# Three passes for a second tile's first product, free clock-warming matmuls, and another order of all operations

## The chip, the cores and the metric

The kernel runs on one core of one Trainium2 chip. The metric is the device time of one execution in microseconds (us), as the median of several runs. Each engine of the core (TensorE, called PE; VectorE, DVE; ScalarE, ACT; GpSimd, POOL) and the queue that issues the transfers (SP) takes its own instructions in the order in which the program gives them; semaphores hold an instruction until what it needs is there.

## The reference

Two layers are applied twice in turn to x of 2048 rows and 640 columns, in float32. The first is an attention over eight earlier rows at distances 0, 2, ... 14, with 32 heads of 20; the second is an MLP with 1536 hidden features. Each is preceded by a layer norm and added to its input.

```
y = layernorm(x)
q, k, v = split(y @ wqkv)                       # 640 -> 3 * 640, 32 heads of 20
logits[s, w] = q[s] . k[s - 2 w] * 20 ** -0.5   # w = 0..7, masked where s - 2 w < 0
x = x + (softmax(logits) . v[s - 2 w]) @ wo
x = x + gelu(layernorm(x) @ w1 + b1) @ w2 + b2  # 640 -> 1536 -> 640
# the same two lines of layers once more, with the same weights
```

## The kernel before, in words

**Tiling.** The rows are split by parity and by halves into four units of 512 rows (`UNITS`); a unit has four tiles of 128 rows. With two layers there are eight unit steps, n = 0 to 7, and the first unit is n = 0. The 640 columns of q, k and v are taken in four groups g of 160.

**Products in two halves.** Each float32 operand is held as a high float16 part and a low float16 part. A product takes three passes: high by high, high by low, low by high (`PASS`), five contraction steps of 128 each, so 15 matmuls for a tile. The high part of a weight slice is made by ACT (line 434) and its low part by DVE (line 435), in `prep_q`; a group of q, k, v has three slices (g, 0), (g, 1), (g, 2).

**The first unit.** Each tile's rows are loaded (line 430), normed on DVE, POOL and DVE again (lines 561 to 563, 566, 606), and split into a high half by ACT (613) and a low half by DVE (615). For tiles 0 and 1 of the first unit PE itself transposes each half with five matmuls against an identity (`turn`, line 489) and ACT copies the result to `yT` (line 497); all other tiles are transposed by a DMA from SP (line 620). Then `qkv` makes the product of the transposed tile with a group's weights (line 654), ACT evicts it (673), and two evicted tiles are put to memory (679), from where `fetch` reads them for the attention (698). The product of tile 0 with group 0 alone is issued in three passes with needs of their own (line 661): the high half by the weights' high parts, then the low half by the high parts, then the high half by the low parts.

**Warming.** Nine operations of eight 128-column matmuls on the identity (`warm`, line 1153) compute nothing that is used. Each needs the identity and, in this kernel, the mean and variance of the first tile; that need is for the planner's order, and the matmuls themselves read the identity alone.

**What sets the order.** The program first lists all operations with engine, needs and buffers (`plan.add`). `Plan.run` then emits them in the order of the list `ORDER`, written out by number; `PLACES` gives the buffer of each use and `BESIDE` a few extra waits. So the order on each engine is fixed by `ORDER`.

Of the kernel before, what the change touches and what calls it, by code (L numbers as in the profile page):

```python
# [261 lines left out]
def sliding_dilated_then_mlp_kernel(  # L262
# [141 lines left out]
    def identity():  # L404
# [7 lines left out]
        give=["b1"])  # L412
# [822 lines left out]
```

## Time and profile before

| | us |
|---|---|
| median of 3 runs (lowest, highest) | 1145.03 (1144.39, 1145.48) |
| the profiled execution's own time | 1144.26 |
| its span, first to last instruction | 1142.5 |
| PE busy in the span | 1134.2 (99%) |
| DVE busy in the span | 1073.7 (94%) |
| ACT busy in the span | 552.5 (48%) |

A row of a timeline gives the start in us, the duration, engine, line, operation, what is written from what, and in brackets the engine's idle time before it and what ended that. Matmuls overlap in the array, so a row's duration is longer than the step from one matmul to the next.

### The profile page before, as it was taken

The numbers are of one execution on the slowest core, as the hardware profiler recorded it, in microseconds if no ns is written. First come the engines' busy times: TensorE is split into PE (matmuls) and PEld (weight loads), VectorE is DVE, ScalarE is ACT, GpSimd is POOL, SyncE is SP. The second block draws the span as 40 slices with busy tenths as digits, with TensorE's granted clock in tenths as the row PEclk, the third lists the DMA queues.
The fourth block names the chain that finished last, engine by engine and source line by source line (L and its number), as shares of the span: only waits on it lengthen the run. The fifth ranks groups of instructions, "written<-read, shape, count | busy, mean of one in ns | idle before, by whom it ended". The sixth has DMA issues, their size and how long they took to land.

```text
span 1142.5 us, 17648 instructions
## 1 busy us (share of the span) xinstructions
PE 1134.2 (99%) x6932; PEld 647.0 (57%) x6932; DVE 1073.7 (94%) x1003; ACT 552.5 (48%) x977; POOL 159.1 (14%) x98
## 2 busy tenths in 40 slices
PE   8999999999999999999999999999999999999998
PEld 5444446577654565445555654556455546566886
DVE  8899999999999999999999999999999999988482
ACT  5476434545364438423645552355447542286360
POOL 2011110311111113100213011121211200300000
PEclk9999999999999999999999999999999999999999
DMA  9999999899976675956475866674598877788856
GB/s 295 324 311 277 278 331 279 262 266 308 240 198 196 216 192 125 253 182 188 155 216 188 179 188 188 213 190 133 164 267 275 258 209 221 211 218 225 251 152 189
DMA packets 259023, 257.38 MB, mean 225 GB/s; under 512 B 138540, under 2 KB 209532, under 8 KB 258940
## 3 DMA queue, kind: packets, MB, share of 16 engines
q1 hardware_dynamic: 258940, 256.26, 78.0%
q8 instruction: 54, 0.88, 0.3%
q14 instruction: 29, 0.24, 0.1%
HBM read 175.64 MB, written 48.71 MB: 196 GB/s over the span
## 4 chain that ended last, share of the span: by engine, by line
PE 99%; DVE 0%; DMA 0%; issue 0%
PE ps L654 34%; PE ps L847 17%; PE acc L866 14%; PE ps L810 11%; PE acc L1124 9%; PE ps L1061 7%; PE acc L869 4%; PE acc L1024 3%; PE ps L1024 1%; PE acc L1153 0%; DMA xf<-in_A_x_dram 0%; PE ps L661 0%; DVE bn L561 0%; PE acc L489 0%; DVE hl L615 0%; DVE bn L562 0%
## 5 line engine op out<-in xcount | busy, mean ns | idle before, releaser
L654 PE MATMUL ps<-wq,yT 128*128 128x480 f16 x1905 | 390.4, 366 | 0.0
L654 PEld LDWEIGHTS <-yT 128*128 128x128 f16 x1905 | 185.6, 98 | 197.0
L847 PE MATMUL ps<-yT,c 128*128 128x512 f16 (+1 forms) x1080 | 204.0, 344 | 0.0
L866 PE MATMUL acc<-c,act 128*128 128x512 f16 x720 | 203.4, 379 | 0.0
L741 DVE TENSOR_TENSOR pr<-qk 128x2560 f32<-128x2560 f32 (+1 forms) x44 | 179.6, 4088 | 0.7
L767 DVE TENSOR_TENSOR pr<-sm,v 128x2560 f32<-128x2560 f32 (+1 forms) x44 | 177.1, 4032 | 0.4
L745 DVE TENSOR_REDUCE sm<-pr 128x128 f32<-128x2560 f32 (+1 forms) x44 | 176.6, 4017 | 0.0
L847 PEld LDWEIGHTS <-c 128*128 128x128 f16 x1080 | 103.8, 98 | 87.4
L673 ACT ACTIVATE ev<-ps 128x480 f32<-128x480 f32 x128 | 70.7, 564 | 162.9 <-PE ps L654 155.5
L869 PE MATMUL acc<-c,act 128*128 128x128 f16 x720 | 148.2, 219 | 0.0
L775 DVE TENSOR_TENSOR pr<-pr 128x2560 f32<-128x2560 f32 (+2 forms) x88 | 143.8, 1645 | 0.2
L810 PE MATMUL ps<-wo,yT 128*128 128x320 f16 x960 | 134.7, 299 | 0.0
L866 PEld LDWEIGHTS <-act 128*128 128x128 f16 x720 | 70.3, 98 | 80.3 <-DVE act L858 0.2
L810 PEld LDWEIGHTS <-yT 128*128 128x128 f16 x960 | 93.0, 98 | 38.1
L590 POOL TENSOR_TENSOR ln<-ln,half 128x2 f32<-128x2 f32 (+1 forms) x30 | 48.6, 1621 | 408.9 <-ACT ln L587 408.9
L1124 PE MATMUL acc<-c,wq 128*128 128x320 f16 x630 | 92.9, 299 | 0.0
L853 ACT ACTIVATE act<-ps,b 128x512 f32<-128x512 f32 (+1 forms) x72 | 43.8, 613 | 93.1 <-PE ps L847 56.0
L624 POOL TENSOR_TENSOR xf<-xf,b 128x640 f32<-128x640 f32 x28 | 58.1, 2085 | 172.9 <-DVE xf L816 36.0
L788 POOL TENSOR_TENSOR ohl<-o,ohl 128x640 f16<-128x640 f32 x24 | 44.3, 1846 | 266.6 <-ACT ohl L786 118.7
L1061 PE MATMUL ps<-yT,c 128*128 128x512 f16 x360 | 78.7, 379 | 0.0
L1124 PEld LDWEIGHTS <-wq 128*128 128x128 f16 x630 | 61.6, 98 | 24.2
L571 ACT ACTIVATE junk<-xf 128x640 f16<-128x640 f32 x56 | 41.1, 733 | 66.8 <-DVE xf L816 54.8
(137 smaller groups left out, 1145.1 us busy)
## 6 DMA issues: line engine op xcount, KB each, us to landing
c<-mw SPq DMA_DIRECT2D x180, 320.0 KB, 4.0
spill<-ev SPq DMA_DIRECT2D x64, 480.0 KB, 5.6
qk<-spill SPq DMA_DIRECT2D x32, 880.0 KB, 5.4
v<-spill SPq DMA_DIRECT2D x32, 880.0 KB, 5.7
c<-msp SPq DMA_DIRECT2D x36, 320.0 KB, 3.6
qk<-spill SPq DMA_DIRECT2D x32, 320.0 KB, 4.8
c<-mw SPq DMA_DIRECT2D x54, 160.0 KB, 3.1
mw<-c SPq DMA_DIRECT2D x24, 320.0 KB, 5.6
```

The lines of the kernel that those rows point to most:

```text
L654: nc.tensor.matmul(ps, transposed(yk)[:, a * KD + k, t * P:(t + 1) * P], wq[:, b, k, g], start=j == 0, stop=j == 3 * KD - 1)
L673: act(3 * GC, -400 + n, lambda i=i, pk=pk, ek=ek: nc.scalar.activation(tile_of(*ek)[:, :, i], tile_of(*pk)[:, :3 * GC].rearrange("p (a c) ...
L741: return nc.vector.tensor_mul(pr(pk), w[:, HALO + m + t0:HALO + m + t0 + TH, None, :].to_broadcast([P, TH, W, GC]), windows(w, t0, [GC, W] ...
L745: dve(E, G - 0.7, lambda pk=pk, t0=t0: nc.vector.tensor_reduce(lg(t0, t0 + TH).rearrange("p t w h -> p (t w h)"), pr(pk).rearrange("p t w ...
L767: return nc.vector.tensor_mul(pr(vk).rearrange("p t w (h d) -> p t (w h) d", d=DH), lg(t0, t0 + TH).rearrange("p t w h -> p t (w h)")[:, : ...
L775: dve(TH * w * GC, G - 0.9, lambda vk=vk, w=w: nc.vector.tensor_add(pr(vk)[:, :, 0:w], pr(vk)[:, :, 0:w], pr(vk)[:, :, w:2 * w]), need=[la ...
L810: nc.tensor.matmul(tile_of(*pk)[:, :D // 2], transposed(yk)[:, a * KD + k, t * P:(t + 1) * P], wo[:, b, k, c * D // 2:(c + 1) * D // 2], s ...
L847: nc.tensor.matmul(tile_of(*pk)[:, :nt], tile_of(*ck)[:, a, k * P:(k + 1) * P], transposed(yk)[:, c * KD + k, t0 * P:t1 * P], start=i == 0 ...
L866: nc.tensor.matmul(acc[i], w, tile_of(*wk)[:, c, :BANK], start=e == 0 and (a, c) == PASS[0], stop=end, skip_group_check=True)
L869: nc.tensor.matmul(acc[4][:, i * P:(i + 1) * P], w, tile_of(*wk)[:, c, BANK:], start=e == 0 and i == t0 and (a, c) == PASS[0], stop=end, s ...
L1061: nc.tensor.matmul(tile_of(*pk), tile_of(*ck)[:, a, k * P:(k + 1) * P], transposed(yk)[:, c * KD + k, :], start=i == 0, stop=i == 3 * KD - 1)
L1124: nc.tensor.matmul(acc[bank][:, :HD], tile_of(*hk)[half][:, a, slot, t * P:(t + 1) * P], load()[:, z, c], start=q in FIRST and i == 0 and ...
```

## The change

The product of tile 1 with group 0 of the first unit is issued in three passes as well, each with its own needs; its 15 matmuls stay 15. The warming operations no longer name the first tile's statistics as a need. `ORDER`, `PLACES` and `BESIDE` are other ones (the operation numbers have moved by two).

```
@@ qkv
-                if n == 0 and g == 0 and t == 0:
+                if n == 0 and g == 0 and t in (0, 1):
...
-                           give=[("qkvp", n, t, g) if c else ("qkvq", a)], use=[pk, yk])
-                        last = [("qkvq", a)]
+                           give=[("qkvp", n, t, g) if c else ("qkvq", t, a)], use=[pk, yk])
+                        last = [("qkvq", t, a)]
...
     for _ in range(WARM):
-        warm([("sq", ("a", 0), 0)])
+        warm([])
...
-ORDER (3529 numbers), PLACES, BESIDE
+ORDER (3531 numbers), PLACES, BESIDE
```

Read with the names of the operations, the two lists begin like this on the engines (t0 and t1 are the tiles, h and l the high and low half, w(g,i) a weight slice):

| engine | before | after |
|---|---|---|
| PE | 4 warm, turn t0h, turn t0l, 5 warm, turn t1h, t0h by h, turn t1l, t0l by h, t0h by l, t1 whole, t2 group 0, t0 group 1 | 9 warm, turn t0h, turn t0l, turn t1h, turn t1l, t0h by h, t1h by h, t0l by h, t1l by h, t0h by l, t1h by l, t2 group 0, t0 group 1 |
| ACT | high of t0, w(0,0), w(0,2), w(0,1), high of t2, high of t1, copy t0h, copy t0l, copy t1h, w(1,0), copy t1l, w(1,1), evict t0, high of t3 | high of t0, w(0,0), w(0,2), copy t0h, high of t1, high of t2, w(0,1), copy t1h, copy t1l, copy t0l, high of t3, w(1,0), w(1,2), w(1,1), evict t1, evict t0 |
| DVE, low parts | t0, w(0,0), w(0,1), t2, t1, w(0,2), w(1,0), t3, w(1,1), w(1,2) | t0, w(0,2), t1, t2, w(0,0), w(0,1), t3, w(1,0), w(1,2), w(1,1) |
| SP | x t0, t1, t2, w(0,0), w(0,2), w(0,1), x t3, w(1,0), w(2,0), x of the next unit, w(1,1), w(1,2), transpose t2 | x t0, t1, t2, w(0,0), w(0,2), w(3,1), w(0,1), x t3, x of the next unit, w(1,2), w(1,1), w(1,0), transpose t2 |

Behind these the operations of all later units are the same ones, exchanged over short distances on every engine.

More of the change, by code (lines that the diff above doesn't have):

```diff
@@ L71 @@
 ORDER = """
[111 rows of a table removed]
[111 rows of a table added]
 """
 PLACES = """
-000000000110000110101032320001111220230203102102132000110303222011120003200121102220011202120002200001001000110100001011000001110010221012110201100111
-010110011012022101012122011201022001001000001100010010010000011001020120120002110100121210001102101202010121202111002200000100100001100100001100001101
-000102112021120011001010100011011212000121202000200112000010010000011010000100100001101012020101220011001102011101001211202021210101021210201000100100
-000110100001001000011010210201210002110001100011001102201102001222010101221020001001000001101000010010000110100012200121000111100111111000020011202120
@@ L190 @@
-101022100011200010010000011010000100100001101011220021000101111002010110011021210100220112001211201000100100000110100001001000011010220010221200212301
-132012012112000002021102002111002021102002111102020102012111002021102012111000002021102002111102020102012111002021102002111102000102112111100000020201
-020121100020211020022111010201020122111010201020022101000000101010201221100101110200221110102010201221210101010201211200000002011102002112102010102012
-112002011102112112002001102202110100000020101222120100010111222020101010101222120100010111222020001102210011102220011232100041212150001100022002100120
@@ L194 @@
-02110022100020211101021212100023211114020205100102002011020020110221100220200011010110000022220200311010140000025200211000022010010220110220
+000000000110000110101302100302111320220001112220130103020020111322020321200121102210021102210022000100100000110001000000010011000110112021210211001101
+011100110110100122210102021210102001001000000111000000100100110100012012012002011110020211011002201000121202010211120020000100100011000100100100001101
+000101212011020110011000110011002100222011120002102220000100010000011010000100100001101012121120021000110012010110011210120201012222012100122000100100
@@ new lines @@
+000110100001001000011010202010211002011001101000110011101002201120012220111000001001000001101000010010000110100120011201101010110111111000021102210021
+012200121212000010010000011010000100100001101011200021201110000102111001001201210120201110122012022000100100000110100001001000011010210121002200212301
+123012012011000001011122102010101020122112010001021122102010101020122012011000001021102002211101020102012211001021102002211101000102212211100000010001
+021122110010011022121110020001022121111020001022021101000000202010220211110201010201211200201110200211210201010201211100000002021102002211101020102012
@@ L195 @@
+211001021102102212101000102112210000000010211021021100020211020021111020101022121100020111022021002100211112000221112230001142210051001200002100100221
+00122100211120000211100022211103020224111005200112000021120000211201201020200021010111000022020200321010141000025000221001002110020021122001
 """
 BESIDE = {
[4 rows of a table removed]
[4 rows of a table added]
 }
```

230 rows, old and new, of tables (BESIDE, ORDER) are left out of this document.

## The prediction

> **What bounds the kernel now.** I read the page first: share of each engine and the chain that ended last.
>
> ```profile
> span 1142.5 us, 17648 instructions
> PE 1134.2 (99%) x6932; PEld 647.0 (57%) x6932; DVE 1073.7 (94%) x1003; ACT 552.5 (48%) x977; POOL 159.1 (14%) x98
> ...
> PE 99%; DVE 0%; DMA 0%; issue 0%
> ```
>
> PE is the bound. The next view is that of PE's waits over the whole span.
>
> ```profile
> PE acc L489 <- ACT hl L613: 2.8, 1, 2.8
> PE acc L1153 <- POOL ident L406: 1.4, 1, 1.4
> PE acc L489 <- DVE hl L615: 0.7, 1, 0.7
> ```
>
> These three are all there are, and the timeline of PE shows where they lie: ahead of 1.35, 7.79 and 8.98 us. From 8.98 us to its last matmul PE never waits.
>
> ```profile
> 1.35 3.60 PE L1153 MATMUL acc<-ident 128*128 128x128 f16 x32 [1.35 <-POOL ident L406]
> 7.79 0.45 PE L489 MATMUL acc<-ident,hl 128*128 128x128 f16 x5 [2.84 <-ACT hl L613]
> 8.98 0.72 PE L489 MATMUL acc<-ident,hl 128*128 128x128 f16 x5 [0.74 <-DVE hl L615]
> 9.49 3.76 PE L1153 MATMUL acc<-ident 128*128 128x128 f16 x40
> 13.08 0.44 PE L489 MATMUL acc<-ident,hl 128*128 128x128 f16 x5
> 13.36 1.18 PE L661 MATMUL ps<-wq,yT 128*128 128x480 f16 x5
> 14.37 0.44 PE L489 MATMUL acc<-ident,hl 128*128 128x128 f16 x5
> 14.65 2.19 PE L661 MATMUL ps<-wq,yT 128*128 128x480 f16 x10
> ```
>
> So the time is the moment at which the first product starts (13.36), plus the PE work behind it, plus a tail. No reordering behind 17 us can gain anything: there is no idle time of PE left to take. It can only lose. The change can gain in the first 13.36 us alone.
>
> The chain in order of time gives the steps without the drain of the array.
>
> ```profile
> 13.53 1.01 PE ps L661 x5
> 14.54 0.28 PE acc L489 x5
> 14.82 2.02 PE ps L661 x10
> 16.84 167.06 PE ps L654 x825
> ...
> 1139.12 0.49 DVE xf L1143
> ```
>
> A 480-column matmul steps by 167.06 / 825 = 0.2025 us, five by 1.01; five transposes cost 0.28, so 0.056 each. One set of transposes (0.28) still stands behind 13.36. **The start that counts** is therefore 13.36 + 0.28 = 13.64: from there, only products follow, without a hole.
>
> **The clock.** PE's granted clock is not the same in these first microseconds. The view of PE by stretches of 3.41 us:
>
> ```profile
> 2.09:5.50 3.41, 2.86 (x27) 2.59 (x25) 1.53 (x5) 0.00 (x0) 0.20 (x1) 1.00 0.89 304
> 5.50:8.92 3.42, 0.45 (x5) 0.28 (x5) 3.28 (x11) 1.61 (x2) 1.88 (x3) 1.00 1.12 324
> 8.92:12.33 3.41, 3.35 (x32) 3.36 (x33) 3.07 (x6) 2.80 (x4) 0.56 (x1) 0.50 1.12 350
> 12.33:15.75 3.42, 3.42 (x37) 2.37 (x35) 3.35 (x7) 3.40 (x7) 0.00 (x0) 1.00 1.34 350
> ```
>
> The first pair of numbers behind the stretch's length is PE's busy time and its matmuls, the third number from the end the clock. A stretch with PE busy for 2.86 was followed by one at 1.00, the stretch with 0.45 by one at 0.50, and 3.35 by 1.00 again. The 32 warming matmuls before 5 us step by some 0.107 (3.60 less the drain, over 32), twice 0.056, so they ran at half clock too, although no event says so. In the kernel before, the half-clock stretch 8.92 to 12.33 falls on warming matmuls, and costs the products nothing but a transpose that starts at 13.08.
>
> **The change, part by part.**
>
> *All 72 warming matmuls first.* They start at 1.35 as before. At 0.107 some 39 are done by 5.50, the other 33 take 33 x 0.056 = 1.85 at full clock: the end is 7.35, ahead of the transposes at 7.79. That costs nothing, and frees PE from 9.4 on.
>
> *When the first product can start.* It needs the high half of tile 0, turned and copied, and the high parts of the three slices of group 0. ACT and SP set this.
>
> ```profile
> 7.81 0.87 ACT L434 ACTIVATE wq<-pr 128x800 f16<-128x800 f32 x1
> 9.13 0.87 ACT L434 ACTIVATE wq<-pr 128x800 f16<-128x800 f32 x1 [0.44 <-DMA pr<-in_A_wqkv_dram]
> 10.40 0.87 ACT L434 ACTIVATE wq<-pr 128x800 f16<-128x800 f32 x1 [0.40 <-DMA pr<-in_A_wqkv_dram]
> 11.18 1.35 ACT L613 ACTIVATE hl<-y 128x640 f16<-128x640 f32 x2
> 12.43 1.87 ACT L497 ACTIVATE yT<-acc 128x640 f16<-128x640 f16 x3
> 14.18 0.88 ACT L434 ACTIVATE wq<-ohl 128x800 f16<-128x800 f32 x1
> ```
>
> The three slices become usable at 7.81, 9.13 and 10.40, some 1.3 apart, and ACT waited for the second and third. In the new order the load of slice (3,1) goes out ahead of the third, (0,1), which so lands one place later: 10.40 + 1.3 = 11.7. ACT meanwhile: conversion at 9.13, free at 9.13 + 0.78 (10.40 to 11.18) = 9.91; a copy takes (14.18 - 12.43) / 3 = 0.58, to 10.49; two high halves take 12.43 - 11.18 = 1.25, to 11.74. The third conversion runs from 11.74 to 12.61, and with the 0.05 from an ACT end to a PE start (7.79 behind 7.74) the first product starts at **12.66**. It is the late slice that costs here: in the old order ACT had it at 11.27.
>
> *No hole behind it at full rate.* The four passes against the high parts take 4 x 1.01, each behind a copy that ACT makes while the pass before it runs: tile 1 high to 13.2, tile 1 low to 13.8, tile 0 low to 14.4, wanted at 13.67, 15.7 and 14.7. The low halves of tiles 1 and 2 follow on DVE behind one conversion of 0.99 (11.03) and ACT's high half (11.2), to 12.7; both sets of tile 1's transposes are done before 12.66. So both sets lie ahead of the start, and the start that counts is 12.66 against 13.64: **0.98 us gained**, if the clock is full.
>
> *The clock at the start.* PE now has no filler between 9.4 and 12.66. In 8.92 to 12.33 it runs three sets of five transposes: 3 x 0.45 = 1.35 us busy as the page counts. The rows give full clock behind 2.86 and half behind 0.45; 1.35 lies below the middle (1.65), so I take the half. The next stretch, 12.33 to 15.75, then holds products from 12.66: 3.09 us at half rate do the work of 1.55, **1.55 us lost**. Bounds: nothing, if 1.35 is enough; 3.09 / 2 and a second stretch of 3.41 / 2 = 1.71, if the first is not judged busy, which the row with 3.35 excludes nearly.
>
> [...]
>
> *The second group's weights.* Slice (1,0) goes from eighth to twelfth place on SP, behind the same number of loads as (1,2) before.
>
> ```profile
> 9.26 2.00 SPq L447 DMA_DIRECT2D ohl<-in_A_wqkv_dram  x2
> 13.05 2.34 SPq L620 DMA_TRANSPOSE yT<-hl  x1
> ...
> DMA to landing us min/median/max: 4.9/6.5/7.9
> ...
> DMA to landing us min/median/max: 5.7/5.7/5.7
> 19.77 1.89 DVE L435 SCALAR_TENSOR_TENSOR wq<-ohl,wq 128x800 f16<-128x800 f32 x2
> ```
>
> The first landing row is of the weight loads, the second of the tile transposes. The twelfth load is issued near 9.76 and lands by 9.76 + 7.9 = 17.7; ACT takes this slice first and the two others queue behind it, so three conversions end at 17.7 + 2 x 0.78 + 0.87 = 20.1, then the evictions of tiles 0 and 1; DVE's last low part comes by some 21.4. PE wants it behind 30 matmuls and a tile: 12.66 + 1.55 + 6.07 + 3.04 = 23.3, so 1.9 us are spare (0.3 at full clock). Tile 2's transpose goes out at 12.8 instead of 13.05 and lands 5.7 later at 18.5; it is wanted at 20.3 (18.7 at full clock). Both cost nothing at half clock; without that cover up to 0.5 us together.
>
> *The other queues and the rest.* POOL's index, zeros and statistics change places within 1 us of work, ahead of nothing that PE needs before 30 us. Two more PE operations are no more matmuls. Behind 17 us PE's order may meet inputs later than before. Bounds: below, nothing (no idle time to win); above, one row shows how near it is.
>
> ```profile
> 230.41 0.42 DVE L858 TENSOR_TENSOR act<-act 128x256 f16<-128x256 f32 x1
> ...
> 231.98 0.38 PE L866 MATMUL acc<-c,act 128*128 128x512 f16 x1
> ...
> DVE hl L615 <- ACT hl L613: 1.2, 1, 1.2
> DVE xf L816 <- PE ps L810: 1.1, 2, 0.7
> DVE wo L435 <- ACT wo L434: 0.3, 1, 0.3
> ```
>
> The low half of the first hidden feature is done at 230.83 and used at 231.98: 1.15 us to spare. The last three rows are all of DVE's idle time between 41 and 233 us, 2.6 us of 192: DVE can't catch up there. An exchange of neighbours costs PE what it delays a DVE result beyond some 1.15; most exchanged steps last 0.4 to 0.8. I take 0, being nearest to what the old order cost, and up to 1.5 for the range.
>
> **The sum.** -0.98 + 1.55 + 0 + 0 = +0.57. Against the profiled execution's own 1144.26 (span 1142.5 and 1.76 around it) that is 1144.83; the median of the runs shown is 0.77 higher, 1145.03, and the same step gives **1145.6**. About 0.2%, 2.3 us, is what a measurement of this kernel can tell from no change, so the forecast is no change.
>
> **The rivals.**
>
> *A: the clock stays full.* If 1.35 us of transposes keep it up, or the stretch falls elsewhere, the gain of 0.98 remains, less up to 0.5 for the weights and the transpose: -0.98 to -0.5, 1144.05 to 1144.5. For it: 1.35 is three times 0.45. Against: it is under half of 2.86, and no row shows a stretch between. This is within 0.2% too. [...]
>
> *B: slower.* DVE comes late to the low halves of the MLP's first features near 232 us, where it has no idle time to recover in, and PE waits for each microsecond beyond 1.15. It decides from a lateness of 1.15; with the 0.57 it passes 2.3 us from a lateness of 2.9. The attention's steps have this size:
>
> ```profile
> 232.89 2.82 DVE L741 TENSOR_TENSOR pr<-qk 128x2560 f32<-128x2560 f32 x1
> ```
>
> One and a half of these ahead of the low halves, 4.2 us, give 0.57 + 4.2 - 1.15 = +3.6, so 1148.6. For it: DVE's order is changed all along from 10 us to the end. Against: in the new list the low halves of features 0 and 1 stand right behind the same maximum of attention group 6 as the first did, and the first attention product has two short steps less ahead of it on DVE.
>
> *C: the change does less than it says.* If PE could not use the earlier start because the third slice lands another 1.3 us later (13.0), the first product starts at 13.9 (13.0 + 0.87 + 0.05), the half-clock stretch still takes (15.75 - 13.92) / 2 = 0.92, and the start that counts is 14.84: +1.2, 1146.2. SP's issue rows show no wait that would do this.
>
> **How the numbers follow.** Forecast 0.50, A 0.25, B 0.10, C 0.10; 0.05 for anything else, most of it a gain beyond A, which no idle time of PE supports. Forecast, A and C are all within 0.2%, with a little of the forecast and C passing 2.3 us when the unknown 1.5 is added: faster 0.04, same 0.84, slower 0.12. The range goes from below A, 1143.6 (0.5 of the runs' own spread under 1144.05), to 1147.3: the forecast with the 1.5 of the later order, rounded up.
>
> **What would show it.** Right: the first product near 12.7, a clock of 0.50 from about 12.3 to 15.7 under it, PE's waits only ahead of about 12.7, and the last matmul about 0.6 later. The clock term is wrong if the first 480-column matmuls step by 0.20; the start is wrong if the third conversion doesn't begin near 11.7; the zero for the rest is wrong if PE's waits have rows behind 20 us. The whole is wrong if the time moves by over 2.3 us.

## The result and the profile after

| | us |
|---|---|
| changed kernel, median of 5 (lowest, highest) | 1156.18 (1155.04, 1156.61) |
| kernel before, beside it, median of 5 | 1144.88 (1144.37, 1145.48) |
| ratio, 95% interval | 1.0099 (1.0085 to 1.0113) |
| the changed kernel's profiled execution, its span | 1155.98, 1154.2 |

The change costs 11.3 us. No change was forecast, and 1156.18 lies outside the range. The page of the changed kernel, the same three lines as were shown of before:

```profile
span 1154.2 us, 17583 instructions
PE 1138.0 (99%) x6932; PEld 646.8 (56%) x6932; DVE 1085.3 (94%) x1003; ACT 553.4 (48%) x979; POOL 160.1 (14%) x98
...
PE 68%; DVE 23%; issue 5%; DMA 2%; ACT 1%; POOL 1%; SPq 0%; DVEq 0%; ACTq 0%
```

Two things are to be seen. VectorE executes the same 1003 instructions, but is busy for 1085.3 us instead of 1073.7. And the chain that ended last, which was TensorE for 99%, now runs over VectorE for 23% of the span. The view of PE's waits behind 17 us, which was empty before:

```profile
PE acc L866 <- DVE act L858: 3.3, 4, 2.0
PE ps L1061 <- ACT ev L1067: 2.1, 1, 2.1
PE ps L810 <- DVE xf L816: 1.4, 3, 1.0
PE ps L1061 <- DMA c<-mw: 1.1, 1, 1.1
PE acc L1124 <- DVE xf L1143: 0.5, 2, 0.2
PE ps L654 <- DMA yT<-hl: 0.3, 1, 0.3
PE ps L810 <- ACT act L853: 0.3, 1, 0.3
```

That is 9.0 us of waits in 13 places, none over 2.1, so no one place is late: VectorE falls behind by a little all along. The view of one stretch shows this best. It goes from VectorE's first product of the attention to its last normalisation of an attention group; the first number is its length, and the third pair is VectorE's busy time and operations. Before:

```profile
41.20:983.14 941.94, 941.94 (x5592) 516.59 (x5591) 930.48 (x753) 450.48 (x815) 139.49 (x78) 1.00 0.78 226
```

After:

```profile
41.26:993.64 952.38, 943.78 (x5577) 515.55 (x5576) 942.61 (x753) 451.95 (x818) 141.80 (x78) 1.00 0.76 222
```

As many operations, 753, take 12.1 us more of VectorE, and the stretch is 10.4 us longer. Behind it both kernels have some 160 us left.

### The profile page after: what moved, and what is told of

Read it like the earlier page. It is cut to its first block, busy times and chain, and to the rows that moved or that the text cites. A ratio compares the mean times of both kernels' runs of the same rounds, so it can differ in the third digit from the quotient of the medians.

```text
span 1154.2 us, 17583 instructions
## 1 busy us (share of the span) xinstructions
PE 1138.0 (99%) x6932; PEld 646.8 (56%) x6932; DVE 1085.3 (94%) x1003; ACT 553.4 (48%) x979; POOL 160.1 (14%) x98
## 4 chain that ended last, share of the span: by engine, by line
PE 68%; DVE 23%; issue 5%; DMA 2%; ACT 1%; POOL 1%; SPq 0%; DVEq 0%; ACTq 0%
PE ps L654 25%; PE ps L847 11%; PE ps L810 8%; PE acc L866 7%; PE acc L1124 7%; DVE sm L745 5%; PE ps L1061 5%; DVE pr L741 4%; DVE pr L767 3%; DVE pr L775 3%; PE acc L1024 3%; PE acc L869 2%; DVE act L858 2%; DVE o L779 1%; DVE hl L615 1%
## 5 line engine op out<-in xcount | busy, mean ns | idle before, releaser
L866 PEld LDWEIGHTS <-act 128*128 128x128 f16 x720 | 70.2, 98 | 83.8 <-DVE act L858 4.6
L590 POOL TENSOR_TENSOR ln<-ln,half 128x2 f32<-128x2 f32 (+1 forms) x30 | 59.3, 1979 | 397.7 <-ACT ln L587 397.7
L869 PEld LDWEIGHTS <-act 128*128 128x128 f16 x720 | 68.2, 98 | 8.0
```

The source lines that it names most:

```text
L866: nc.tensor.matmul(acc[i], w, tile_of(*wk)[:, c, :BANK], start=e == 0 and (a, c) == PASS[0], stop=end, skip_group_check=True)
L869: nc.tensor.matmul(acc[4][:, i * P:(i + 1) * P], w, tile_of(*wk)[:, c, BANK:], start=e == 0 and i == t0 and (a, c) == PASS[0], stop=end, s ...
```

## What VectorE's added time is made of

The trace shows two things that lengthen VectorE's work without adding an operation. The timeline of one place, VectorE first and GpSimd's work (POOL) below it: the addition of a bias (624) and the subtraction that makes a low half of the attention's output (788), both called adds here. After:

```profile
546.78 0.42 DVE L750 TENSOR_TENSOR sm<-sm,mask 128x256 f32<-128x256 f32 x1
547.24 0.62 DVE L753 TENSOR_REDUCE sm<-sm 128x32 f32<-128x256 f32 x1
547.89 0.42 DVE L754 TENSOR_TENSOR sm<-sm 128x256 f32<-128x256 f32 x1
548.24 0.48 DVE L816 SCALAR_TENSOR_TENSOR xf<-ps,xf 128x320 f32<-128x320 f32 x1
548.64 3.73 DVE L858 TENSOR_TENSOR act<-act 128x512 f16<-128x512 f32 x2
552.29 5.47 DVE L745 TENSOR_REDUCE sm<-pr 128x256 f32<-128x5120 f32 x1
...
548.46 1.55 POOL L624 TENSOR_TENSOR xf<-xf,b 128x640 f32<-128x640 f32 x1 [1.83 <-DVE sm L754]
549.96 1.85 POOL L788 TENSOR_TENSOR ohl<-o,ohl 128x640 f16<-128x640 f32 x1
```

Before, near the same place:

```profile
545.92 0.69 DVE L858 TENSOR_TENSOR act<-act 128x512 f16<-128x512 f32 x1
546.52 0.48 DVE L816 SCALAR_TENSOR_TENSOR xf<-ps,xf 128x320 f32<-128x320 f32 x1
546.92 0.61 DVE L753 TENSOR_REDUCE sm<-sm 128x32 f32<-128x256 f32 x1
547.44 0.88 DVE L816 SCALAR_TENSOR_TENSOR xf<-ps,xf 128x320 f32<-128x320 f32 x2
548.24 0.42 DVE L754 TENSOR_TENSOR sm<-sm 128x256 f32<-128x256 f32 x1
548.57 5.48 DVE L745 TENSOR_REDUCE sm<-pr 128x256 f32<-128x5120 f32 x1
...
548.80 1.54 POOL L624 TENSOR_TENSOR xf<-xf,b 128x640 f32<-128x640 f32 x1 [2.24 <-DMA qk<-spill]
550.30 1.40 POOL L788 TENSOR_TENSOR ohl<-o,ohl 128x640 f16<-128x640 f32 x1
```

**Dependent neighbours.** After, the maximum (753) starts 0.46 us behind the mask (750) whose result it needs, 0.04 after that one's end; the subtraction (754) 0.65 behind the maximum, 0.03 after its end. Before, another operation stands behind the maximum and starts 0.52 behind it, ahead of its end by 0.09. Over the whole stretch of the changed kernel an operation directly behind one whose result it needs starts on average 0.034 us after that one's end, any other 0.08 us before it: 0.114 us for each such pair. By the needs in the list, the kernel before has 75 such pairs among its neighbours on VectorE, the changed one 153; in the stretch 35 and 116.

**Adds beside VectorE.** The low half (858) takes 0.69 us before, and two of them take 3.73 after, because GpSimd's two adds run at the same time; the second ends at 552.37, 0.56 us behind the end of the second add. Before, the same two adds run beside the long reduction (745), which takes 5.48 with them and 5.47 without. Adds have to wait for an operation that the table `BESIDE` names for them. The table names the same operations in both kernels, but in the new order of VectorE something else stands behind the named operation: a long reduction 12 times instead of 19, a low half 15 times instead of 2. Operations over 0.3 us longer than the median of their form, all of them beside an add and called stretched from here on: in the stretch 7 with 8.1 us together before, 12 with 14.4 after.

Lying beside an add is not enough; the order of the starts matters. Every stretched operation of the two kernels between 41 and 995 us has two inputs and begins while an add is running, and it is longer by what that add had left, less some 0.14 us, at most by 1.35. (Some that begin so are not stretched.) An operation that began with no add running, and in which one then began, is not longer: 31 of them before and 34 after, none over 0.01 us above the median of its form; there the add can be. One place before shows both:

```profile
598.38 5.48 DVE L741 TENSOR_TENSOR pr<-qk 128x5120 f32<-128x5120 f32 x1
603.78 2.03 DVE L858 TENSOR_TENSOR act<-act 128x512 f16<-128x512 f32 x1
...
598.54 8.68 POOL L624 TENSOR_TENSOR xf<-xf,b 128x640 f32<-128x640 f32 x2 [19.18 <-DVE sm L760]
```

The product (741) began first and takes its usual 5.48. The row of GpSimd holds two adds; the first, begun 0.16 us after the product, takes 6.72 alone, instead of 1.54. The low half (858; its two inputs both lie in the buffer `act`) begins while that add still runs, and takes 2.03 instead of 0.69.

So the sum for the stretch is 81 pairs x 0.114 = +9.2, stretched operations +6.3, idle time of VectorE (gaps over 0.15 us) 9.0 before and 4.4 after, -4.7, and operations that moved in or out -0.5: +10.3, against 10.4 measured. The experiments test whether these are causes, and how much each takes.

## The experiments

### Head or tail

**head_of_after** has the changed head (the first 19 operations of PE, 14 of ACT, 20 of VectorE and 13 of SP, with the three passes for tile 1) and behind it the order, the buffers and the waits of before; **tail_of_after** has the head's operations in the order of before, and the changed order behind.

```diff
 head_of_after, against before
-                if n == 0 and g == 0 and t == 0:
+                if n == 0 and g == 0 and t in (0, 1):
...
-        warm([("sq", ("a", 0), 0)])
+        warm([])
...
-ORDER, the head's numbers
+ORDER, the head's numbers of the changed kernel
```

> The changed kernel's own head (three passes for tile 1, all warming matmuls first, its order of the first 19 PE, 14 ACT, 20 DVE and 13 SP operations), and the order, buffers and extra waits of before behind it. Theory 1 (the new order of DVE behind the head costs the time: it puts operations that need each other's result next to each other, 153 pairs against 75, and DVE is never idle from 41 to 930 us): the head is harmless, the first product starts near 12.3 as in the changed kernel, the time is 0 to 0.9 us under before, 1144.0 to 1144.9. Rival 2 (the head costs: the split product, the cold clock or the late weight slices set off the later waits): the loss of 11 us stays, 1153 to 1157. Rival 3 (it is the order of the other engines or of the transfers behind the head): same as theory 1 here.

> The complement to the head alone: the head in the order of before (warming matmuls split around the first transposes, tile 1's product in one piece of 15, slice (0,1) third among the weight loads), and behind it the changed kernel's order and buffers. Theory 1 (the order behind the head costs, by DVE's neighbours): the whole loss is here, 1155 to 1157. Theory 1b (the order behind the head costs, by results that come late from one engine to the other): the same. Rival 2 (the head costs): about before, 1144 to 1147.

Measured: head_of_after 1144.94 us, ratio 1.0001 (0.9992 to 1.0011); tail_of_after 1157.53, ratio 1.0113 (1.0098 to 1.0128). The whole loss comes from the order behind the head; tail_of_after lies 0.5 above its range.

### VectorE's order put back alone

```diff
 after_dve_of_before, VectorE's operations alone, against the changed kernel
-55 23 50 57 39 ...
+55 17 20 57 50 ...
```

> The changed kernel with one engine's order changed: DVE takes its operations in the order of before as far as the needs and buffers of the others allow (41 of 979 stand elsewhere, by 13 places at most; 85 pairs of neighbours need each other). Theory 1: DVE's busy time falls back by about (153 - 85) x 0.117 = 8 us, and the time with it, to 1146 to 1149. Rival 2 (the head costs) and rival 3 (ACT, POOL, SP or PE order costs): 1154 or more, since all of these stay as in the changed kernel.

Measured: 1246.53 us, ratio 1.0889 (1.0871 to 1.0907). The expectation failed. The orders of the engines are made to fit each other, and one put back alone leaves the others waiting, as the first row of PE's waits shows:

```profile
PE ps L654 <- ACT ev L673: 38.4, 9, 9.2
```

So VectorE's order can't be judged by exchanging it whole. The next kernels exchange neighbours only.

### Swapping neighbours without a look at who waits

```diff
 before_more_pairs, VectorE's operations alone, against before: 75 swaps, dependent neighbours 75 -> 153
-96 260 258 261
+96 258 260 261
```

```diff
 before_neutral_swaps, against before: 69 swaps, dependent neighbours stay 75
-105 96 260 258 261
+105 260 96 258 261
```

> The kernel before with 75 exchanges of two neighbours in DVE's order and nothing else changed; each exchange puts an operation directly behind the one whose result it needs. Pairs that need each other rise from 75 to 153, as many as in the changed kernel; no operation moves by more than one place; all exchanges lie between 41 and 583 us. Theory 1: each pair costs 0.117 us of DVE (0.034 gap instead of 0.083 overlap), so DVE is some 9 us longer busy, and the time rises by 7 to 9 us, to 1152 to 1154. Rivals 2 and 3 (or distances by which operations have moved): no operation has moved, no head, no other engine: within 1 us of before.

> The control to the exchanges: the kernel before with 69 exchanges of two neighbours in DVE's order at about the same places, chosen so that the number of pairs that need each other stays 75. Theory 1: within 1 us of before. If any exchange of neighbours costs (results late by one place), it is as slow as the kernel with more pairs, 1152 or more.

Measured: 1160.16 (1.0133, 1.0118 to 1.0148) and 1165.7 (1.0179, 1.0164 to 1.0194). The control lost more than the test, so the pair of runs decides nothing: swaps without regard to slack make results late, as one row of the control's PE waits shows.

```profile
PE acc L866 <- DVE act L858: 8.1, 3, 6.6
```

### Swapping neighbours with 1.5 us to spare

Only those neighbours are swapped whose results and inputs have at least 1.5 us to spare in the trace (1.0 in gentle_less). gentle_more makes dependent pairs (75 to 168, 85 swaps), gentle_more_half every second of them (to 120, 42 swaps), gentle_same leaves their number (84 swaps), and gentle_less takes pairs out of the changed kernel (153 to 109, 40 swaps).

```diff
 gentle_more, against before
-258 261 259 429
+258 259 261 429
```

```diff
 gentle_same, against before
-266 283 267 268
+266 267 283 268
```

```diff
 gentle_more_half, against before
-262 111 263 284
+262 263 111 284
```

```diff
 gentle_less, against the changed kernel
-435 3 260 261
+435 260 3 261
```

> The kernel before with 85 exchanges of two neighbours in DVE's order between 41 and 930 us. Each puts an operation directly behind one whose result it needs (pairs 75 to 168, so 93 more). Unlike in the first pair of exchanges, only such neighbours are exchanged where, by the trace of before, every other engine and transfer that waits for the delayed one starts at least 1.5 us later than it would then be done, and the inputs of the advanced one are there 1.5 us before. Theory 1: 93 x 0.114 = 10.6 us more of DVE work, the time up by 9 to 12 us, 1154 to 1157. Theory 1b (late results alone count): within 2 us of before, since nothing comes late by an exchange.

> The control by the same rule: 84 exchanges of neighbours in DVE's order of before, at least 1.5 us to spare at each, pairs that need each other unchanged at 75. Theory 1: within 2 us of before. If it is 8 us or more slower, exchanges as such cost, whatever their neighbours, and the count of pairs explains nothing.

> About half the dose: 42 of the exchanges of neighbours by the rule with 1.5 us to spare, pairs 75 to 120 (45 more; 93 more cost 9.1 us). Theory 1 (each pair costs DVE the same, one after the other): 45 x 0.098 to 0.114 = 4.4 to 5.1 us, 1149 to 1150. If the cost comes from a few single places, it is far from half: under 1147 or over 1152.

> The changed kernel with 40 exchanges of neighbours in DVE's order that take an operation away from behind the one whose result it needs (pairs 153 to 109), by the same rule with 1.0 us to spare. Theory 1: 44 x 0.114 = 5.0 us less of DVE work, the time 4 to 6 us under the changed kernel, 1150 to 1152. Theory 1b: within 2 us of the changed kernel's 1156.2.

Measured: gentle_more 1153.74 (1.0079, 1.0064 to 1.0094), gentle_more_half 1149.15 (1.0039, 1.0025 to 1.0052), gentle_same 1144.81 (1.0001, 0.9991 to 1.0010), gentle_less 1152.41 (1.0072, 1.0054 to 1.0089). As many swaps cost nothing when they leave the pairs alone; 85 and 42 swaps cost 9.1 and 4.5 us when they make 93 and 45 pairs. gentle_more lies 0.3 under its range and gentle_less 0.4 above. The same stretch of VectorE, gentle_more:

```profile
41.00:992.60 951.60, 943.87 (x5592) 516.67 (x5591) 943.19 (x753) 449.48 (x815) 144.64 (x78) 1.00 0.78 224
```

gentle_same:

```profile
41.28:983.36 942.08, 942.08 (x5592) 516.79 (x5591) 930.77 (x753) 450.71 (x815) 136.46 (x78) 1.00 0.78 226
```

This looked like the whole cause, but it isn't: the swaps of gentle_more had also put adds beside short operations, 12 stretched ones between 41 and 995 us instead of 9, and 14 instead of 9 over the whole span. A swap can't change one without the other; that had to be taken apart later.

### As few dependent pairs as the slack allows

```diff
 after_fewest_pairs, against the changed kernel: 51 moves, pairs 153 -> 91
-435 3 260 261
+435 260 3 261
```

```diff
 before_fewest_pairs, against before: 9 moves, pairs 75 -> 66
-267 268 286 273 433
+267 433 268 286 273
```

```diff
 head_fewest_pairs, against head_of_after: 8 such moves, pairs 75 -> 67
-269 270 288 275 435
+269 435 270 288 275
```

> The changed kernel with 51 moves in DVE's order, by up to five places, that part operations which need each other (pairs 153 to 91, 62 fewer; between 41 and 930 us), 0.8 us to spare by its trace. Theory 1: 62 x 0.09 to 0.114 = 5.6 to 7.1 us less, 1149 to 1151; what is left above before, some 4 to 6 us, is the 16 pairs that stay and the waits of the new order. If the pairs were only a part that other waits give back, no better than the 40 exchanges, 1152.4.

> The kernel before with 9 moves in DVE's order that part operations which need each other (75 to 66), 0.5 us to spare. Theory 1: 9 x 0.1 = 0.9 us less on DVE; but PE has no idle time behind the head, so it can't end earlier than its work: no change, within 0.5 us of before. If DVE alone set the end, 0.9 us faster.

> The changed kernel's head with the order of before behind it, and 8 moves that part operations on DVE which need each other (75 to 67). PE's products can start up to 1.4 us earlier when the clock stays full, and DVE has 0.8 us less to do. Theory 1: 0.3 to 1 us under before where the clock stays full in the head and none where the half-clock stretch falls on the first products: 1143.9 to 1144.9 in the median. It can't be told from no change unless it is over 1 us.

Measured: after_fewest_pairs 1151.23 (1.0056, 1.0040 to 1.0071), before_fewest_pairs 1144.76 (1.0000, 0.9991 to 1.0009), head_fewest_pairs 1145.1 (1.0006, 0.9997 to 1.0015). 62 pairs less gave 5.0 us back, short of the expected 5.6. head_fewest_pairs, expected up to 1 us under before, shows no change. With 16 pairs more than before the kernel is still 6.6 us slower than before: pairs can't be all of it.

### The adds alone

The order of every engine stays as it is; only the operation behind which an add starts is another one. (The expectations say 44 entries; the table has 49.)

```diff
 after_beside, against the changed kernel: 18 entries, to the operation ahead of a long reduction
 BESIDE
-402: 540, 499: 203, 1029: 1142
+402: 2046, 499: 512, 1029: 2452
```

```diff
 after_fewest_beside, against after_fewest_pairs: 15 entries
-402: 540, 545: 554, 1029: 1142
+402: 2046, 545: 2106, 1029: 1144
```

```diff
 before_beside_bad, against before: 9 entries, so that a short operation with two inputs begins while the add runs
-400: 538, 405: 555, 742: 752
+400: 536, 405: 554, 742: 2252
```

> The changed kernel with every engine's order untouched; only the table that says behind which VectorE operation a GpSimd add starts is written anew for 18 of its 44 entries, so that the adds that ran beside stretched VectorE operations start together with one of the long reductions instead. Theory 2 (the adds stretch VectorE's two-input operations by 1.1 to 1.35 us each, 12 times between 41 and 995 us): VectorE's time in stretched operations there falls from 14.4 us to under 4 us, some of which comes back as idle time as in the earlier runs, so the time falls from 1156.2 by 4 to 9 us, to 1147-1152. Rival (only the dependent neighbours cost; the adds' places are covered): 1155.5-1157.

> The changed kernel with 51 VectorE operations moved (91 dependent neighbours instead of 153) and, in addition, 15 entries of the table for the GpSimd adds written anew in the same way. If dependent neighbours and GpSimd adds together are the whole loss, the time is that of the kernel before within 1.5 us: 1144-1147. Rival (a third cause keeps the rest): 1149-1151.5, as with the 51 moves alone (1151.2).

> The kernel before with every engine's order untouched; only 9 entries of the table for the GpSimd adds are written anew, so that these adds start just ahead of a short two-input VectorE operation instead of with a long reduction. Dependent neighbours stay at 75. Theory 2: each stretches one VectorE operation by 1.1 to 1.35 us, VectorE's busy time grows by 8 to 12 us, and the time by what its 9 us of idle time do not take: 1148-1156. Rival (covered): 1144-1146.

Measured: after_beside 1147.46 (1.0023, 1.0014 to 1.0033), after_fewest_beside 1146.58 (1.0017, 1.0007 to 1.0026), before_beside_bad 1151.73 (1.0061, 1.0044 to 1.0078). The first and the third are as theory 2 expects, one each way. after_fewest_beside is within its range of 1144 to 1147, but 2.0 us above before, not within the 1.5 that would have made the two causes the whole loss. In after_beside the place shown above looks like this (its lines are numbered three lower), the two low halves at 1.29 instead of 3.73:

```profile
549.85 1.29 DVE L855 TENSOR_TENSOR act<-act 128x512 f16<-128x512 f32 x2
551.05 5.48 DVE L742 TENSOR_REDUCE sm<-pr 128x256 f32<-128x5120 f32 x1
...
551.28 1.54 POOL L621 TENSOR_TENSOR xf<-xf,b 128x640 f32<-128x640 f32 x1 [3.43 <-DVE act L855]
552.78 1.40 POOL L785 TENSOR_TENSOR ohl<-o,ohl 128x640 f16<-128x640 f32 x1
```

Its stretch is back at 941 us although all 116 pairs are still in it:

```profile
43.20:984.30 941.10, 940.39 (x5578) 515.46 (x5577) 930.21 (x753) 451.55 (x817) 141.56 (x78) 1.00 0.77 225
```

before_beside_bad, whose orders are those of before:

```profile
41.92:990.98 949.06, 943.67 (x5592) 516.73 (x5591) 939.21 (x753) 449.83 (x815) 131.65 (x78) 1.00 0.77 224
```

### The pairs alone, the kernel before with room on VectorE, and the head with it

```diff
 gentle_more_level, against gentle_more: 4 entries
-278: 298, 405: 555, 410: 724, 497: 203
+278: 865, 405: 698, 410: 2196, 497: 393
```

```diff
 before_beside, against before: 14 entries, to operations ahead of long reductions; head_beside has the same against head_of_after
-326: 163, 718: 728, 831: 942
+326: 478, 718: 2232, 831: 2400
```

> gentle_more (the kernel before with 85 neighbours on VectorE swapped, 168 dependent neighbours instead of 75) with 4 of the 44 entries for the GpSimd adds written anew, so that the adds that came to lie beside stretched operations only through the swaps start with a long reduction again. Theory that both causes are real: the added dependent neighbours are 93 x 0.11 = 10.2 us of VectorE's time, stretched operations stay at the 9 or 10 of the kernel before, and idle time takes 4 to 6 us of it: 1148.5-1151.5. Rival (dependent neighbours cost nothing; gentle_more lost its 9.1 us to the adds alone): 1144.3-1146.5.

> The kernel before with every order untouched and 14 entries for the GpSimd adds written anew, so that they start with long reductions; its 9 stretched operations between 41 and 995 us fall to 3 or fewer, VectorE's busy time by 6 to 8 us. Theory that TensorE bounds the kernel before and VectorE's work counts only from some us above it: no change, 1143.5-1145.3, and VectorE's idle time grows by what its busy time loses. Rival (VectorE is the bound in the kernel before too): faster by 3 us or more, under 1142.

> The changed kernel's head with the orders of the kernel before behind it (head_of_after, 1144.94 us), and the same 14 entries as in before_beside. If VectorE had swallowed the 0.9 us by which the new head starts its products earlier, they reach the end now: 1143.2-1144.4. If TensorE alone bounds both and the half clock under the first products takes the gain: 1144.5-1145.3, as head_of_after.

Measured: gentle_more_level 1148.56 (1.0035, 1.0021 to 1.0049), before_beside 1144.5 (1.0000, 0.9991 to 1.0009), head_beside 1145.14 (1.0004, 0.9995 to 1.0012). The pairs cost 3.8 us by themselves, with 9 stretched operations between 41 and 995 us as before; the rest of gentle_more's 9.1 us was the adds', or came of both together. before_beside takes 6.2 us of VectorE's time away, and the length of the stretch does not move:

```profile
41.94:983.87 941.93, 941.93 (x5592) 516.71 (x5591) 924.25 (x753) 451.73 (x815) 128.42 (x78) 1.00 0.77 226
```

So TensorE bounds the kernel before, but VectorE stands right beneath it. No version is faster than the kernel before.

### The runs in one table

The second column is the difference to the median of before, measured beside it; then the dependent neighbours of the whole list, the stretched operations between 41 and 995 us with what they lose, and from the stretch from the first attention product to the last normalisation its length and VectorE's busy time, all in us. Two of before's nine stretched operations lie behind its stretch.

| kernel | against before | pairs | stretched | length | VectorE busy |
|---|---|---|---|---|---|
| before_beside | -0.3 | 75 | 3 (3.4) | 941.9 | 924.3 |
| after_fewest_beside | +2.0 | 91 | 2 (2.2) | 942.0 | 925.1 |
| after_beside | +2.9 | 153 | 3 (3.0) | 941.1 | 930.2 |
| before | 0 | 75 | 9 (10.5) | 941.9 | 930.5 |
| gentle_same | +0.2 | 75 | 10 (10.9) | 942.1 | 930.8 |
| after_fewest_pairs | +6.6 | 91 | 12 (14.0) | 947.0 | 936.8 |
| gentle_more_half | +4.5 | 120 | 11 (13.3) | 945.6 | 937.2 |
| gentle_less | +7.8 | 109 | 11 (13.4) | 947.5 | 937.7 |
| gentle_more_level | +3.8 | 168 | 9 (9.8) | 946.1 | 938.0 |
| before_beside_bad | +7.1 | 75 | 15 (17.2) | 949.1 | 939.2 |
| tail_of_after | +12.9 | 153 | 13 (14.7) | 952.3 | 942.5 |
| after | +11.3 | 153 | 12 (14.4) | 952.4 | 942.6 |
| gentle_more | +9.1 | 168 | 12 (13.7) | 951.6 | 943.2 |

Sorted by VectorE's busy time, the table has a knee. Up to 931 us the stretch lasts 941 to 942, whatever VectorE does: TensorE sets it. From 937 on the length is the busy time and 8.2 to 10.2 us. The two lines meet where VectorE is busy for 932 to 934 us, 1.3 to 3.3 us above the kernel before.

The other seven kernels are not in the table. The three with the new head and before_fewest_pairs are within 0.5 us of before, with VectorE busy for 930 us or less. The three that were changed without regard to slack don't lie on the second line: in before_more_pairs the stretch is 16.8 us longer than VectorE's busy time, in before_neutral_swaps 24.9, in after_dve_of_before 73.0. There single late results cost time that the busy time doesn't show.

The four kernels with the changed order make the two causes visible together:

| | adds as changed | adds beside long reductions |
|---|---|---|
| 153 pairs | 1156.18 | 1147.46 |
| 91 pairs | 1151.23 | 1146.58 |

Neither effect adds to the other simply: moving the adds gives 8.7 us with all the pairs and 4.7 with few, taking pairs out gives 5.0 and 0.9. Each works only as far as VectorE is above the knee. The rest of 2.0 us in after_fewest_beside isn't in the stretch. In its profiled execution a half-clock stretch lies under the first products (the clock, third number from the end, is 0.51), which costs 1.7 us, half of its 3.41:

```profile
13.55:16.96 3.41, 3.41 (x10) 1.32 (x9) 3.34 (x8) 1.33 (x4) 1.23 (x1) 0.51 1.33 230
```

In that execution the products start 0.6 us ahead (13.08 against 13.64), and PE waits twice, which delays it by 1.0: together 2.1 of the 2.2 us by which its span is longer. How it is in the other executions, 1144.16 to 1149.84 us, no run shows; for the median this rest stays open.

## Why the prediction was wrong, step by step

**"From 8.98 us to its last matmul PE never waits", so reordering "can only lose".** Both true, and the second half was the warning. From "PE is the bound" I went on as if VectorE's work behind 17 us were free as long as no result came late by itself. The step that failed is the term for **the other queues and the rest: 0, and up to 1.5 for the range**. It measured +12.9 us in tail_of_after, and +11.3 with the new head; the sign named for it, rows of PE's waits behind 20 us, was there. What was missing was the sum: VectorE had 11.5 us without work in 941.9 of the stretch, and of these 8 or more stayed in every row of the table, so anything beyond 1.3 to 3.3 us of added work went to the end. The three rows of idle time that I quoted, 2.6 us in 192, said this. I used them to price one late result, not the engine's work.

**"Most exchanged steps last 0.4 to 0.8"** treated an exchange as a delay that is over when both have run. An exchange of neighbours also changes what each costs: 0.114 us for each pair that becomes dependent, and up to 1.35 us for an operation with two inputs that comes to begin while an add is running. I read the table of waits as the same one with its numbers moved by two, and it names the same operations; their neighbours had changed.

The order of the starts matters, and so does what runs beside the add. Low halves, which have two inputs, were stretched by up to 1.35 us where the add had begun first; the product at 598.38, begun ahead of the add, took its usual 5.48, and the add 6.72 instead of 1.54. The reductions have one input and are not longer in either order: 16 before and 17 after begin between 41 and 995 us while an add is running, none over 0.011 us above the median of its form, and the one at 548.57, begun ahead of its adds, took 5.48 beside them and 5.47 without. The 53 adds of the two kernels that begin during a reduction take 1.39 to 1.56, their usual time. What in the chip makes this difference, no run shows.

**Rival B (slower)** had the engine right: VectorE without time to recover in, low halves (858) late, TensorE waiting. It had neither the mechanism nor the place nor the size: not one lateness near 232 us, 1148.6, but added work over 940 us.

**The start.** The first product was to start at 12.66; in the profile it is 12.26, since the third conversion began at 11.36, not 11.74:

```profile
8.74 0.87 ACT L434 ACTIVATE wq<-pr 128x800 f16<-128x800 f32 x1 [0.34 <-DMA pr<-in_A_wqkv_dram]
10.10 1.35 ACT L613 ACTIVATE hl<-y 128x640 f16<-128x640 f32 x2
11.36 0.85 ACT L434 ACTIVATE wq<-pr 128x800 f16<-128x800 f32 x1
12.26 6.24 PE L661 MATMUL ps<-wq,yT 128*128 128x480 f16 x30
```

ACT set it, as predicted: no wait for a load stands ahead of 11.36. The steps were right, and the whole chain lay 0.4 us earlier in this execution; in three other kernels with this head the first product started at 12.40, 12.87 and 13.08. Rival C (a third slice later still) didn't come.

**The clock.** In this execution it stayed full, as rival A has it:

```profile
6.73:10.14 3.41, 2.10 (x34) 1.75 (x31) 3.27 (x9) 2.90 (x5) 1.77 (x2) 1.00 1.15 337
10.14:13.55 3.41, 2.19 (x17) 1.27 (x18) 3.34 (x7) 3.41 (x7) 0.00 (x0) 1.00 1.09 369
```

In head_of_after, with the same head, the half-clock stretch came where it was forecast, under the first products, behind a stretch with PE busy for 1.09. The products start 1.24 us ahead there (12.40 against 13.64) and lose 1.27 (half of 12.40 to 14.94), the two terms of the forecast:

```profile
8.12:11.53 3.41, 1.09 (x14) 0.58 (x11) 3.34 (x6) 3.30 (x6) 1.21 (x1) 1.00 1.11 361
11.53:14.94 3.41, 3.05 (x12) 1.56 (x13) 3.34 (x8) 2.41 (x4) 1.06 (x1) 0.50 1.11 359
```

The edges of these stretches are at 5.50, 8.92 and 12.33 in before, at 6.73 in after, at 11.53 and 14.94 here (10.14 and 8.12 are counted from them by 3.41): another place in each of the three executions. Of the forecast loss of 1.55 us, 1.27 stand in this execution and nothing in the changed kernel's.

**The head as a whole.** Where the clock stays full, the products reach the transposes early. I had put up to 0.5 us on tile 2's and the weights together; tile 2's cost 0.3 in the changed kernel. In head_beside it is tile 3's (issued at 20.23, the product behind it starts at 26.41), which I had not looked at, and the wait is 1.2, PE's only one behind 14 us:

```profile
PE ps L651 <- DMA yT<-hl: 1.2, 1, 1.2
```

There the products start at 12.87, 0.77 ahead of the 13.64 of before, and the wait takes more than that. The sum of the head, no change, was right: head_of_after is at 1.0001 and head_beside at 1.0004. No wait of PE for the second group's weights stands in a profile, as predicted. But in head_beside the chain ahead of that 1.2 us runs over their last load (issued at 9.69, landed at 17.69), so they may have a share in it; no run separates this.

## What to carry to other kernels

A bound engine without waits says nothing about how far the next engine is from becoming the bound (here 1.3 to 3.3 us): take that engine's busy time in the stretch, add what the change puts on it, and compare with the length less the idle time that remained even where it was the bound (here 8 to 10 of 942 us). The reordering put 12.1 us of work on VectorE in the stretch although no operation was added: count the neighbours that become dependent (here 0.114 us for each pair), and see which operations with two inputs come to begin while an add of GpSimd is running (here up to 1.35 us for each). A wait that places one engine's work by naming another engine's operation is only as good as what stands behind that operation, and has to be made again with each new order.

## What the runs showed of the hardware

- Two-input operations of VectorE that began while an add of GpSimd was running took up to 1.35 us longer (a low half 2.03 instead of 0.69 at 603.78 before). None of the operations that began with no add running, and in which one then began, was longer by over 0.01 us, but the add could be (6.72 instead of 1.54 beside the product at 598.38). One-input reductions beside adds were not longer, whichever began first (at most 0.011 us for the 33 that began second; 5.48 against 5.47 for a long one that began first).
- In the changed kernel's stretch from 41.26 to 993.64 us an operation of VectorE started on average 0.034 us after the end of its neighbour if it needed that one's result, and 0.08 before the end if not.
- A single wait of TensorE for 2.0 us was followed by a whole stretch at half clock in the changed kernel, which made it cost 1.7 us more (10 matmuls in 3.41 us instead of 19). The stretch with that wait had PE busy for 1.43 of 3.41 us:

```profile
566.44 0.57 PE L866 MATMUL acc<-c,act 128*128 128x512 f16 x1 [1.98 <-DVE act L858]
```

```profile
563.11:566.52 3.41, 1.43 (x9) 0.62 (x8) 3.38 (x5) 0.04 (x1) 0.00 (x0) 1.00 0.44 125
566.52:569.93 3.41, 3.41 (x10) 1.23 (x11) 3.41 (x3) 3.24 (x6) 0.00 (x0) 0.50 0.92 257
569.93:573.34 3.41, 3.41 (x19) 1.64 (x18) 3.38 (x4) 0.52 (x1) 0.00 (x0) 1.00 0.13 20
```

The length of the wait alone didn't decide it here. The granted clock changes at 566.52, 569.93 (3.413 later) and 1153.61 (171 times 3.413 later). A wait of 2.05 us, ended at 940.20, lies across 938.57, which is 109 such steps behind 566.52: PE is busy for 2.99 us in the step ahead of 938.57 and for 1.78 in the one behind it, and the clock stays at 1.00 after both.

The changed kernel's span is 11.7 us longer. By the starts of its matmuls, against their usual steps, the 13 waits delay PE by 11.0 (the view of waits gives 9.0, some 0.16 less for each) and the half-clock stretch by 1.7; the products start 1.4 ahead (12.26 against 13.64). That makes 11.3 and leaves 0.4 open.
